# A planned attention-then-feed-forward kernel: two gate units in turns, one weights piece and the decays behind the second unit's rows, waiting engines, filler products and late fills

## The chip, the cores and the metric

The kernel runs on one core of a Trainium2 chip. The metric is the device time of one execution in microseconds. The kernel before took 734.04 us (median of 3 runs, 733.62 to 735.03).

## The reference

Two blocks follow each other. The first is a gated linear recurrence for 4 batches, 8 heads, 768 steps and head size 48; the second is a SwiGLU feed-forward on 3072 tokens of 384 features with a hidden width of 1536.

```python
mag = np.sqrt(a_re * a_re + a_im * a_im)
scale = np.minimum(mag, 0.999) / (mag + 1e-06)
a_re_n, a_im_n = (a_re * scale, a_im * scale)
for t in range(S):
    ar, ai = (a_re_n[:, :, t, :, None], a_im_n[:, :, t, :, None])
    new_re = ar * S_re - ai * S_im
    new_im = ar * S_im + ai * S_re
    kv = np.einsum('bhd,bhe->bhde', k[:, :, t], v[:, :, t])
    S_re, S_im = (new_re + kv, new_im)
    y[:, :, t] = np.einsum('bhd,bhde->bhe', q[:, :, t], S_re)
...
xn = x / np.sqrt(np.mean(x * x, axis=-1, keepdims=True) + 1e-06) * rms_g
g = xn @ w_gate
silu = g * (1.0 / (1.0 + np.exp(-g)))
return (silu * (xn @ w_val)) @ w_out
```

## The kernel before

The sequence is cut into 24 chunks of 128 steps (`N = 24`, n = 0 to 23). Chunks are grouped twice: into gate units (`UNITS`: chunk 0, chunk 1, then pairs) and into feed-forward groups of two chunks (`GROUPS`).

For a unit, `gates(u)` loads a_re and a_im (`load_gates`, tiles `in`) and q and k (`load_kq`, tile `kin`), works out in three stages ("size", "root", "turn") the running magnitude and angle of the decay (ScalarE table functions and VectorE scans over tiles `t`, `in`, `turns`), turns q and k by them into `rot`, and moves the rows of `rot` by six DMAs of 128 KB into a head-by-head layout, `kq`. Six small DMAs more move the chunk's end magnitudes, `ends`, into `decay`. `moved[n]` is the list of the row DMAs of chunk n.

For a chunk, `attend(n)` forms scores from `kq` on TensorE in small 32-column products (banks 4 and 5), masks them into `am` (`copy_predicated`), multiplies by v (`ve`) and by the carried state, and updates `state` with the chunk's decay. The stage "norm" squares the result (`sq`), sums it by a product with `ones`, takes the power -0.5 on GpSimd (`rs`), spreads it by another product, and writes `xT`, the normalised input of the feed-forward.

For a group, `feed(g, xT)` multiplies by w_gate (`wg`) and w_val (`wv`) in six blocks of 4 x 6 products, applies Silu on ScalarE (`sg`), multiplies on VectorE (`hT`), and multiplies by w_out (`wo`). From group 2 on the last product uses seven half-size products instead of eight (`weight_sums`).

The weights come in 64-bit words, as 12 pieces: 0 to 5 are w_gate and w_val in turns (1536 KB each), 6 to 11 are w_out (768 KB each). `fetch` loads a raw piece from GpSimd's DMA queue into free room in `wo` or `hT`; `narrow(i)` makes fp32 of it with one ScalarE instruction and three VectorE instructions. At most two pieces are in flight (`AHEAD`), the first waits until the gate inputs of unit 0 have landed (a one-element GpSimd copy, `junk`), and by `CLEAR = {3: 0}` piece 3 also waits until the rows of chunk 0 have landed (the copy `seen<-kq`).

Nothing of this is issued in program order. Each helper (`tt`, `act`, `dma`, `mms` and so on) only records an operation in `Flow`, with a planned duration and with what it reads and writes. `Flow.dates` works a due time backwards from the feed-forward products (`clock`), and `Flow.schedule` runs through time and gives every free engine, among the operations whose inputs are ready, the one due earliest. `behind` keeps a DMA's issue after that of others. The result is a fixed order for each engine, which `issue` writes out; all instructions therefore have line 648 in the profile, and they are told apart by their tiles. On the chip each engine takes its own list strictly in order, with the waits that reads and writes ask for. In the order that is written out, each DMA of the SP queue also waits until the one eight before it on the hardware queues has landed.

```python
key = o["due"]
if o["table"] and table not in self.TABLES[o["table"]]:
    key += self.switch
if pick is None or key < pick[0]:
    pick = (key, o)
```

The steps that the texts below speak of are found at `narrow` and `fetch` (pieces), `load_gates` and `load_kq` (inputs of a unit), `gates` with its last loop (the decays), `attend` with its "norm" stage, and the block of `fill` calls near the top of `fast` (constants and zeros, mostly on GpSimd). The names `kq`, `decay`, `am`, `state` in the profile leave out the buffer number: even chunks use the first buffer, odd chunks the second.

Of the kernel before, what the change touches and what calls it, by code (L numbers as in the profile page):

```python
# [19 lines left out]
C = 128  # L20
# [441 lines left out]
class Flow:  # L462
# [7 lines left out]
    LAND = 2.0  # L470
    LANES = 8
    BEGIN = {"SP": 0.8, "ACT": 0.8, "POOL": 0.8}
    TABLES = {"silu": ("S",), "sin": ("S", "T"), "arctan": ("T",), "rsqrt": ("A",)}

    def __init__(self, nc, rooms):
        self.nc = nc
        self.rooms = rooms
        self.ops = []
        self.seen = {}
        self.stage = None  # L480
        self.shift = {}

    def box(self, ap):
# [17 lines left out]
    def note(self, op, ap, write):  # L501
        b = self.box(ap)
        if b is None:
            return
        name, p0, p1, lo, hi = b
        if name.startswith("bank"):
            p0, p1, lo, hi = 0, P, 0, 2048
        kept = []
        for x in self.seen.get(name, ()):
            o, w, q0, q1, l, h = x  # L510
            over = q0 < p1 and p0 < q1 and l < hi and lo < h
            if over and (write or w) and o != op["i"]:
                op["deps"].add(o)
            if not (write and p0 <= q0 and q1 <= p1 and lo <= l and h <= hi):
                kept.append(x)
        kept.append((op["i"], write, p0, p1, lo, hi))
        self.seen[name] = kept

    def add(self, eng, calls, dur, reads=(), writes=(), table=None, land=None, due=None, after=(), behind=()):
        op = dict(i=len(self.ops), eng=eng, calls=calls, dur=dur, deps=set(), table=table, land=land,  # L520
                  base=due, stage=self.stage, behind={o["i"] for o in behind})
        self.ops.append(op)
        op["deps"].update(o["i"] for o in after)
        for ap in reads:
            self.note(op, ap, False)
        for ap in writes:
            self.note(op, ap, True)
        return op

    def dates(self):  # L530
# [15 lines left out]
        for op in self.ops:  # L546
            op["due"] += self.shift.get(op["stage"], 0.0)
        return users

    def schedule(self):  # L550
# [4 lines left out]
        waiting = {}  # L555
        table = None
        for op in self.ops:
            free.setdefault(op["eng"], self.BEGIN.get(op["eng"], 0.0))
            waiting.setdefault(op["eng"], [])
            if not left[op["i"]]:  # L560
                waiting[op["eng"]].append(op)
# [21 lines left out]
        while True:  # L583
# [26 lines left out]
            for o in waiting[eng]:  # L610
                if ready[o["i"]] > t + 1e-9:
                    continue
                key = o["due"]
                if o["table"] and table not in self.TABLES[o["table"]]:
                    key += self.switch
                if pick is None or key < pick[0]:
                    pick = (key, o)
            o = pick[1]
            waiting[eng].remove(o)
            dur = o["dur"]  # L620
            if o["table"] and table not in self.TABLES[o["table"]]:
                table = self.TABLES[o["table"]][-1]
                dur += 1.3
                self.loads = getattr(self, "loads", 0) + 1
            if eng == "PE":
                busy = sum(min(e, t) - max(b, t - 4.0) for b, e in recent if e > t - 4.0)
# [18 lines left out]
    def issue(self):  # L645
        for op in sorted(self.ops, key=lambda o: o["order"]):
            for fn, args, kw in op["calls"]:
                fn(*args, **kw)  # L648


def fast(tc, ctx, qT, kT, v, a_re, a_im, w_gate, w_val, w_out, rms_g, out, H, bad):
# [192 lines left out]
    for t, x in ((ones, 1.0), (halfpi, PI / 2), (mid, -(RE_MAX + RE_MIN) / 2),  # L844
                 (width, -(RE_MAX - RE_MIN) / 2), (mhalf, -0.5), (zeros, 0.0)):
        fill(t, x)
    for t in ves + states:
        fill(t[:, :, :, D:], 0.0)
    add("POOL", [(make_identity, (nc, ident), {})], 0.6, [], [ident])
    fill(causal, 1.0)  # L850
    for e in range(2):
        for b in range(4):
# [3 lines left out]
                                                            base=-BLK * (3 - b if e else b),  # L856
                                                            channel_multiplier=-1))], 0.3, [x], [x])
    for t in ams:
        fill(t, 0.0)
    for t in banks[4:6]:  # L860
# [21 lines left out]

    CLEAR = {3: 0}

# [61 lines left out]
    HOLD = 1  # L946
    begun = []
    cleared = {}
    loaded = {}
# [31 lines left out]
    def load_kq(u, t):  # L981
        flow.stage = "kq", u
        for name, ap in (("q", qT), ("k", kT)):
            for i, n in enumerate(UNITS[u]):
                dma(t[name][:, :, i * C:(i + 1) * C],
                    ap[n].rearrange("d (h t) -> (d h) t", t=C).rearrange("(j p) t -> p j t", p=P),
                    behind=moved[HOLD] if u > 1 else rows_)
        return t

    def gates(u):  # L990
# [45 lines left out]
        tt(q, q, t4)  # L1036

        flow.stage = "turn", u
        act(im, im, AF.Arctan, after=[root])
        last = turn.get(u - 1) if ns[0] % NCH else None  # L1040
# [16 lines left out]
        for i, n_ in enumerate(ns):  # L1057
            cs = slice(i * C, (i + 1) * C)
            for a, f in enumerate((t5, t3)):
                tt(rots[n_ % 2][:, a * ND:(a + 1) * ND].rearrange("p j (o t) -> p j o t", t=C), t["kq"][:, :, :, cs],  # L1060
                   f[:, :, cs].unsqueeze(2).to_broadcast([P, ND, 2, C]))
        for n_ in ns:
            moved[n_] = [dma(kqs[n_ % 2][r:D2:2 * ND], rots[n_ % 2][:, r], "SP") for r in range(2 * ND)]
            if n_ < 2:
                cleared[n_] = copy(seen, kqs[n_ % 2][:, 0, 0:1], eng="POOL")
        for r in range(2 * ND):
            dma(decays[way_of(u)][r:D2:2 * ND], ends[:, r % ND, ns[0]:ns[0] + nt], behind=moved[ns[0]])

# [9 lines left out]
    def attend(n):  # L1078
# [3 lines left out]
        vv = vns[0]  # L1082
        later = dict(behind=moved[min(n - 1, HOLD)] if n else ())
        rows = v[n * C:(n + 1) * C, :].rearrange("t (m e d) -> t m e d", e=2, d=D)
# [6 lines left out]
        for a in range(2):  # L1091
# [3 lines left out]
            for h in range(HH):  # L1095
                for b in range(4):
                    c = 3 - b if h % 2 else b
                    list_.append((s[c * BLK:(c + 1) * BLK, h, b * BLK:], k[:, a * HH + h, b * BLK:(b + 1) * BLK],
                                  q[:, a * HH + h, b * BLK:], True, True))
            mms(list_, HH // 2 * 0.29, due=EARLY.get(n))  # L1100
            pairs = lambda t: t.rearrange("s (m e) t -> s m e t", e=2)
# [21 lines left out]
        order = [lines[c][i] for i in range(len(lines[0])) for c in range(4)]  # L1123
        mms(order, len(order) * mm_time(C) / 4 * 1.1 + 0.15)
        if not last:
            kt = kts[0]
            for a in range(2):
# [8 lines left out]
            mms([(st[c * BLK:(c + 1) * BLK, h], kt[:, h, c * BLK:(c + 1) * BLK], vv[:, h], True, True)  # L1136
                 for h in range(H) for c in range(3)], H * 0.1)
            st4 = ps.rearrange("p (m e d) -> p m e d", m=NP, e=2)
# [44 lines left out]

    FIRST = 2
    B = {(k, j): wo[:, k * HD:(k + 1) * HD, j * DH:(j + 1) * DH] for k in range(2) for j in range(2)}
    blocks = lambda t: t.rearrange("p (f c) -> p f c", f=HD)
# [85 lines left out]
    for u in range(2):  # L1272
        load_kq(u, loaded[u])
    gates(0)
    gates(1)
    for i in range(len(pieces)):
        narrow(i)
    gated = 2
    for n in range(N):
        while gated < NU and UNITS[gated][0] <= n:  # L1280
            gates(gated)
            gated += 1
# [15 lines left out]
    for in_, limit, op in ((ef, P_MIN, ALU.is_ge), (ef, 1.0, ALU.is_le), (range_, 0.0, ALU.is_le),  # L1298
# [12 lines left out]
        0.2, [ps[0:1, 0:1]], [], due=clock[0] - 15.0)  # L1311

    flow.schedule()
    with tc.manual_schedule():
# [51 lines left out]
```

## Time and profile before

| what | value |
|---|---|
| median of 3 runs | 734.04 us |
| profiled execution, its own time | 735.44 us |
| its span from first to last instruction | 733.7 us |
| TensorE busy | 679.7 us (93%) |
| VectorE busy | 473.2 us (64%) |
| ScalarE busy, of it 68 table loads | 331.3 us, 87.2 us |
| GpSimd busy | 42.0 us |
| moved by DMA | 80.64 MB |

A row of the profile gives engine, operation, output tile and input tiles, and shape; times are from the start of the span. "SPq" and "POOLq" are the DMA-issuing instructions of the queues. In the timeline the number in front is the start, the next one the length, and a bracket tells how long the engine had been idle before and what released it. In a window row each engine has its busy microseconds and, in brackets, its instructions; PEclk is TensorE's granted clock, the last two columns are the share in use of the 16 DMA engines and GB/s. A TensorE product of fp32 is two records in the profile.

### The profile page before, as it was taken

What the parts mean: (1) busy time and instruction counts of PE and PEld (TensorE: products, weight loads), DVE (VectorE), ACT (ScalarE), POOL (GpSimd) and SP (SyncE); (2) the same over time, 40 slices, a digit from 0 to 9 for tenths busy, and PEclk for the clock granted to TensorE, in tenths of its full rate; (3) what the DMA queues carried; (4) which work ended last, traced back from release to release, by engine and by line L of the source; (5) the groups of instructions that cost most, each with busy time, mean ns of one, the idle gap of its engine ahead of it and who ended that gap; (6) DMA issues with size and microseconds to landing.
All of it is one profiled execution on the core that took longest, in us unless ns stands there. A gap on an engine that the chain in (4) does not pass through costs nothing.

```text
span 733.7 us, 16076 instructions
## 1 busy us (share of the span) xinstructions
PE 679.7 (93%) x6842; PEld 598.6 (82%) x6842; DVE 473.2 (64%) x740; ACT 331.3 (45%) x451; POOL 42.0 (6%) x80
## 2 busy tenths in 40 slices
PE   0269989999999999999999999999999999999996
PEld 0257866877888889889889889889889889889885
DVE  6979897789798887886856745765845233234121
ACT  7646856867384742841832732731830110111010
POOL 5122200000000000000000001000000000000000
PEclk9978999999999999999999999999999999999999
DMA  8597675544756625643523303313303202200000
GB/s 296 186 318 211 163 178 160 140 128 110 195 129 152 177 84 139 215 145 78 151 66 77 119 22 73 113 34 79 106 1 77 66 13 67 65 12 3 22 0 27
DMA packets 104575, 80.64 MB, mean 110 GB/s; under 512 B 42800, under 2 KB 95280, under 8 KB 104496
## 3 DMA queue, kind: packets, MB, share of 16 engines
q1 hardware_dynamic: 100432, 64.99, 33.2%
q0 software_dynamic: 3264, 14.16, 5.6%
q8 instruction: 56, 0.92, 0.5%
q10 hardware_dynamic: 800, 0.39, 0.2%
q14 instruction: 23, 0.19, 0.1%
HBM read 55.84 MB, written 4.72 MB: 83 GB/s over the span
## 4 chain that ended last, share of the span: by engine, by line
PE 64%; DVE 2%; DMA 2%; SPq 2%; ACT 1%; issue 0%; DVEq 0%; ACTq 0%
PE bank L648 64%; SPq L648 2%; DMA kq<-rot 1%; DMA in<-in_a_im_dram 1%; DVE turns L648 0%; DVE t L648 0%; ACT turns L648 0%; DVE hT L648 0%; DVE large L648 0%; DVE xT L648 0%; DVE in L648 0%; ACT L648 0%; DVE small L648 0%; DVE ot L648 0%; DVE rot L648 0%
## 5 line engine op out<-in xcount | busy, mean ns | idle before, releaser
L648 PE MATMUL bank<-xT,wg 128*128 128x256 f32 x864 | 200.8, 382 | 2.8 <-DVE xT L648 2.8
L648 PE MATMUL bank<-xT,wv 128*128 128x256 f32 x864 | 199.0, 380 | 0.0
L648 PEld LDWEIGHTS bank<-xT,wg 128*128 128x128 f32 x864 | 164.4, 191 | 25.9 <-DVE xT L648 3.5
L648 PEld LDWEIGHTS bank<-xT,wv 128*128 128x128 f32 x864 | 163.6, 190 | 22.5
L648 PE MATMUL bank<-wo,hT 128*128 128x192 f32 (+1 forms) x576 | 124.8, 360 | 0.5 <-DVE hT L648 0.4
L648 DVE TENSOR_TENSOR hT<-bank,sg 128x512 f32<-128x512 f32 x72 | 49.4, 687 | 108.6 <-PE bank L648 104.9
L648 PEld LDWEIGHTS bank<-wo,hT 128*128 128x128 f32 x576 | 94.6, 190 | 14.2 <-issue 1.4
L648 ACT ACTIVATE sg<-bank 128x512 f32<-128x512 f32 x72 | 42.8, 595 | 133.3 <-PE bank L648 132.9
L648 ACT ACT_TABLE_LOAD x68 | 87.2, 1283 | 16.3 <-DVE rot L648 8.6
L648 PE MATMUL bank<-kq 96*32 96x96 f32 (+3 forms) x1536 | 35.5, 243 | 33.8 <-DVE wg L648 28.2
L648 PEld LDWEIGHTS bank<-kq 96*32 96x32 f32 x1536 | 31.7, 114 | 39.7 <-DVE wg L648 28.2
L648 DVE TENSOR_TENSOR rot<-kin,turns 128x768 f32<-128x768 f32 x48 | 44.9, 953 | 18.4 <-DMA kq<-rot 17.5
L648 ACT ACTIVATE sq<-bank 128x384 f32<-128x384 f32 x24 | 11.7, 487 | 96.5 <-PE bank L648 95.8
L648 POOL TENSOR_TENSOR rs<-ssv,mhalf 128x1 f32<-128x1 f32 x24 | 18.4, 766 | 573.1 <-DVE ssv L648 573.1
L648 ACT ACTIVATE kt<-bank 128x384 f32<-128x384 f32 x40 | 18.4, 486 | 64.4 <-PE bank L648 63.6
L648 PE MATMUL bank<-sums,hT 128*128 128x192 f32 x240 | 45.2, 330 | 0.0
L648 PE MATMUL bank<-am,ve 128*32 128x128 f32 x768 | 41.4, 290 | 0.4 <-DMA ve<-in_v_dram 0.4
L648 PEld LDWEIGHTS bank<-sums,hT 128*128 128x128 f32 x240 | 39.4, 190 | 0.4 <-DVE mid L648 0.3
L648 DVE TENSOR_TENSOR hT<-hT 128x768 f32<-128x768 f32 x40 | 38.2, 954 | 0.9
L648 DVE COPY_PREDICATED am<-causal,bank 128x512 f32<-128x512 int32 x48 | 32.9, 720 | 8.1 <-PE bank L648 8.1
L648 ACT ACTIVATE turns<-in 128x768 f32<-128x768 f32 (+1 forms) x39 | 29.9, 789 | 14.8 <-DVE in L648 11.0
L648 PE MATMUL bank<-kq,state 96*32 96x128 f32 x640 | 35.6, 285 | 0.0
(110 smaller groups left out, 715.6 us busy)
## 6 DMA issues: line engine op xcount, KB each, us to landing
kq<-rot SPq DMA_DIRECT2D x144, 128.0 KB, 2.4
kin<-in_q_dram SPq DMA_DIRECT2D x24, 192.0 KB, 3.1
kin<-in_k_dram SPq DMA_DIRECT2D x24, 192.0 KB, 4.4
wo<-in_w_gate_dram SPq DMA_DIRECT2D x6, 768.0 KB, 4.4
out_dram<-ot SPq DMA_DIRECT2D x24, 192.0 KB, 2.2
wo<-in_w_val_dram SPq DMA_DIRECT2D x6, 768.0 KB, 5.0
wo<-in_w_out_dram SPq DMA_DIRECT2D x6, 768.0 KB, 4.7
in<-in_a_re_dram SPq DMA_DIRECT2D x11, 384.0 KB, 4.5
```

What stands on the lines that cost most here:

```text
L648: fn(*args, **kw)
```

## The change

- **Gates in turns.** `gates` becomes a generator that stops once, after the root stage. For units 0 and 1 the first part of both is recorded, then the second part of both; the angle function (`Arctan`, another table) of each waits for the roots of both.
- **Piece 3 behind the second rows.** `CLEAR` is `{3: 1}`: the fourth weights piece waits for the rows of chunk 1 instead of chunk 0.
- **Decays behind the second rows.** The decay DMAs of units 0 and 1 are recorded after unit 1's rows and placed behind them in the SP queue; those of later units follow their own unit's second rows (`send_decays`).
- **Waiting engines.** When the planner has picked an operation for ScalarE or VectorE, and one due over 50 us earlier becomes ready within 1.5 us, while the picked one would still run, the engine idles until then.
- **Fillers.** Up to 62 us of planned time, gaps of TensorE are filled with products of 128 x 128 by 128 from the first `rot` into bank 3, after the first `rot` instruction. 38 of them are issued: 16 ahead of the scores of chunk 0, 7 and 8 around the second half of the scores of chunk 1, and 2, 4 and 1 in the norm stage of chunk 1.
- **Late fills.** Fills of `ve`, `state`, `am`, the mask and the identity are due no earlier than 12 us.
- **Planner details.** Loads of q, k and v of one unit or chunk do not count as dependent on each other (`group`); a change between product shapes costs 0.06 us of planned time (the rate for ordering by it, `turn`, stays 0); two planned durations of products are changed.

The program contains the same operations otherwise, in a new order on every engine. On VectorE the two units' first parts now stand ahead of the first `rot`, and between the masks of chunk 0 and those of chunk 1 the order is: piece 1, one of the three instructions of piece 2, `state<-bank,decay`, the other two of piece 2. On ScalarE the list before the squares of chunk 1 holds the first instruction of unit 2 (`t<-in`) and the conversion of piece 3, in that order. The program has as many table loads as before.

```diff
+            if eng in self.patient:
+                for x in waiting[eng]:
+                    if t < ready[x["i"]] < t + o["dur"] - 0.2 and x["due"] < o["due"] - 50.0 and ready[x["i"]] < t + 1.5:
+                        pick = None
+                        free[eng] = max(free[eng], min(ready[y["i"]] for y in waiting[eng] if t < ready[y["i"]]))
+                        break
+                if pick is None:
+                    continue
...
+            if eng == "PE" and o["mode"] != mode:
+                mode = o["mode"]
+                dur += 0.06
+            if eng == "PE" and self.warm and t < self.warm["until"]:
+                since = max([free["PE"]] + [x["end"] + self.SYNC for x in self.warm["after"] if not recent])
+                n = int((t - since - 0.3) / 0.43)
+                if n > 0:
+                    self.fillers.append((order - 0.5, n))
+                    recent.append((since, since + 0.43 * n))
...
+    LATE = 12.0
     for t in ves + states:
-        fill(t[:, :, :, D:], 0.0)
+        fill(t[:, :, :, D:], 0.0, late=LATE)
...
-    CLEAR = {3: 0}
+    CLEAR = {3: 1}
...
+    def send_decays(u):
+        ns = UNITS[u]
+        for r in range(2 * ND):
+            dma(decays[way_of(u)][r:D2:2 * ND], ends[:, r % ND, ns[0]:ns[0] + len(ns)], behind=moved[max(ns[0], 1)])
...
+        roots.append(root)
+        yield
         flow.stage = "turn", u
-        act(im, im, AF.Arctan, after=[root])
+        act(im, im, AF.Arctan, after=roots[-2:])
...
-        for r in range(2 * ND):
-            dma(decays[way_of(u)][r:D2:2 * ND], ends[:, r % ND, ns[0]:ns[0] + nt], behind=moved[ns[0]])
+        if u:
+            for x in (u - 1, u) if u == 1 else (u,):
+                send_decays(x)
...
-            mms(list_, HH // 2 * 0.29, due=EARLY.get(n))
+            mms(list_, HH // 2 * 0.285, due=EARLY.get(n), mode=BLK)
...
-        mms(order, len(order) * mm_time(C) / 4 * 1.1 + 0.15)
+        mms(order, len(order) * mm_time(C) / 4 * 1.06, mode=BLK)
...
-    gates(0)
-    gates(1)
+    firsts = [gates(0), gates(1)]
+    for x in firsts * 2:
+        next(x, None)
...
+    filler = rots[0][:, 0]
+    flow.warm = dict(after=started, until=WARM, call=[
+        (nc.tensor.matmul, (banks[3][:, 0:C],), dict(lhsT=filler[:, 0:C], rhs=filler[:, C:2 * C], start=True, stop=True))])
```

## The prediction

> **What bounds the kernel now.** First the page's busy shares by slice and what TensorE waited for:
>
> ```profile
> PE   0269989999999999999999999999999999999996
> ```
>
> ```profile
> PE bank L648 <- DVE wg L648: 28.2, 1, 28.2
> PE bank L648 <- DMA kq<-rot: 5.6, 2, 4.8
> PE bank L648 <- DVE am L648: 5.2, 2, 3.2
> ```
>
> From the fourth slice on TensorE is full; all its long waits are before. So whatever brings the start of the full stretch forward moves the end with it, as long as nothing behind goes empty. (The wait of 28.2 us is put down to `wg`, but the copy `seen<-kq` begins at 28.20: the rows of chunk 0 ended it.) Then the windows, with busy time of PE, PEld, DVE, ACT, POOL, PEclk, DMA share, GB/s:
>
> ```profile
> 25.00:30.00 5.00, 1.78 (x56) 1.81 (x60) 4.96 (x6) 2.88 (x8) 0.44 (x1) 1.00 0.37 89
> 40.00:45.00 5.00, 1.04 (x32) 1.07 (x36) 3.52 (x3) 1.63 (x1) 2.23 (x4) 0.65 0.96 299
> 45.00:50.00 5.00, 4.56 (x86) 3.79 (x81) 4.18 (x6) 0.49 (x1) 1.65 (x3) 0.50 1.11 293
> 55.00:60.00 5.00, 3.51 (x53) 2.99 (x54) 4.96 (x6) 4.79 (x8) 1.83 (x2) 0.52 0.55 112
> 80.00:85.00 5.00, 5.00 (x25) 4.38 (x25) 4.98 (x7) 4.96 (x8) 1.68 (x3) 1.00 0.37 91
> 95.00:100.00 5.00, 3.87 (x74) 2.25 (x72) 5.00 (x8) 3.26 (x4) 0.00 (x0) 1.00 0.82 220
> ```
>
> DMA is idle around 25 to 30 and full from 40 to 50; TensorE's clock is half there; VectorE is full from 55 to 100, while TensorE runs feed 0. Then single steps, in the timelines:
>
> ```profile
> 33.03 4.18 SPq L648 DMA_DIRECT2D kq<-rot  x6
> 43.96 2.36 PE L648 MATMUL bank<-kq 96*32 96x128 f32 x64 [4.78 <-DMA kq<-rot]
> 50.27 0.84 ACT L648 ACTIVATE t<-in 128x768 f32<-128x768 f32 x1 [2.58 <-DMA in<-in_a_re_dram]
> 58.65 3.62 PE L648 MATMUL bank<-xT,wg 128*128 128x256 f32 x8
> 90.95 1.82 DVE L648 TENSOR_TENSOR rot<-kin,turns 128x768 f32<-128x768 f32 x2
> 98.01 1.33 PE L648 MATMUL bank<-kq 96*32 96x128 f32 x64 [0.82 <-DMA kq<-rot]
> 101.83 0.55 PE L648 MATMUL bank<-ident,kq 96*128 96x96 f32 x4 [2.01 <-DVE am L648]
> ```
>
> Chunk 1's rows, issued up to 37.2, land at 43.9, while piece 3 (POOLq from 30.83) flows. Feed 0 starts at 58.65. At 98.0 TensorE waits for unit 2's rows, which VectorE finished in `rot` at 92.77: **from 58 to 98 VectorE, not TensorE, sets the pace**, and a feed 0 that starts earlier pays only as far as `rot` of unit 2 comes earlier.
>
> **What the skill says.** (1) "TensorE: Matmul & The Clock Gate", What's actually happening: after some 3.4 us of idleness the clock halves, and as long a busy time restores it. The trace agrees: the 64 score products took 2.36 us at 43.96 and 1.33 us at 98.01. (2) "DMA: Bandwidth & Descriptors", Issuing engines are not separate DMA queues: all queues share the 16 engines and interleave. It agrees: the 12 row DMAs of 20 to 50 us took 2.2 to 7.6 us to land, the slow ones beside a piece. (3) "SBUF — State Buffer", Who interferes with whom: a two-port VectorE operation and GpSimd block each other. It agrees: two 384-element TENSOR_SCALARs took 1.46 us at 8.54, one took 0.33 at 11.08; GpSimd was filling until 10.04.
>
> **The change, part by part**, on the execution with a span of 733.7 us.
>
> *Gates in turns, to the rows of chunk 0.* ScalarE starts at 4.72 as before, but the square of unit 0's a_im is now behind five instructions instead of two: three more at some 0.42 us each, and one dependent gap. On VectorE 0.96 + 0.56 + 0.51 of unit 1 stand before unit 0's scans, so these end at about 12.1 (before 11.16). Roots and square: 12.2 to 13.7, one table load to 15.0 (before two, 12.30 and 14.13), angle of unit 0 at 15.0 (13.59). Then VectorE: two corrections, two `kin`, scan, two corrections of unit 1, one step to 18.3, with the conversion of piece 0 (1.6) on ScalarE until 18.8; magnitude 0.5, load 1.28, sine and cosine 1.0: 21.6 (20.03). First `rot` 22.6 to 23.5 (22.02 before), second to 24.4 (24.34, since no unit 1 step lies between). Six row DMAs at 0.68 each from 23.6: the last is issued at 27.0 (25.6), rows land at **29.6 (28.2): a loss of 1.4**. The late fills cost nothing: GpSimd ends its fills near 10.1 as before, and VectorE's TENSOR_SCALAR now comes after that, which saves the 0.8 us lost at 8.54; that is in the dates above. The first wait for ACT's inputs moves by 0.2 (the table load now precedes the DMAs), hidden behind a_re, which ScalarE waits for until 4.72.
>
> *Rows of chunk 1.* VectorE's `rot` of unit 1 ends at 30.2 (before 33.9). SP has `kq` 0 until 27.6, four `ve` until 30.2, then six rows until 34.3 (before 37.2). Nothing of 1.5 MB flows beside them, so 2.5 us after the last issue, as with chunk 0: **36.5 against 43.9, a gain of 7.4**.
>
> *Decays.* Queued behind the rows: six from 34.9 to 38.8, landing after 1.8 to 5.9 us (the spread of the 12 of before): 41 is taken, 44 the upper end. `state<-bank,decay` waits for them on VectorE, free at 38.4; behind it are queued 1.76 + 1.76 of piece 2 and the masks of chunk 1: these end at 46.4 (before 47.1). So 6 of the 7.4 are lost again here.
>
> *Piece 3.* It waits on GpSimd's queue, where piece 4 (at 38.3, before 39.11) and the powers (from 45) stand behind it and lose nothing. Issued at 36.9 (30.83), landed by a rate as before (9.5 us): 46, at most 49. Unit 2's a_re is issued at 38.9 (41.14) and takes 9.1 us as before: 48. ScalarE stands at its first instruction for this, 0.84, then the conversion of piece 3, 1.6: the square of chunk 1 can start at 50.4 (53.16). Its result y, masks at 46.4, power product and 2 us at a warm clock (114.47 to 116.4; cold it took 4.8), is ready at 48.9, so the input sets the date. From the square 0.5, sum 0.7, `ssv` 0.2, power 0.7 to 1.2, product 0.5, `xT` 0.55 and handovers: **feed 0 starts at 54.2 (58.65): 4.4 earlier**; 52.3 if a_re lands at 46, 56 if at 50.
>
> *Fillers.* A record of 128x256 takes 2.75/12, less its tail, 0.216 warm, 0.43 cold; a filler is two records half as wide, 0.22 warm, 0.43 cold. The first 16 end between 27.1 and 30.5, 29.0 taken, ahead of the rows (29.6): at worst 0.9 on a path that has slack at `decay`. Those between scores fill waits. What they gain is in y above (2.8 of 4.8); feed 0 also lost 1.7 by the clock (91.46 - 58.65 less 72 x 0.432), but that is before VectorE's date and counts nothing.
>
> *VectorE from `xT` to `rot` of unit 2.* In before 57.74 to 92.77: 35.0. The list after is the same less one `hT` product (0.6), plus the first two instructions of piece 4 (0.95 + 1.76), which were done earlier: 33 us of lengths if nothing is waited for, 34.8 with a wait for a_im of unit 2 until 55. So `rot` 102 ends at 87.3 to 88.9, mean 88.3 against 92.77; rows land 5.2 later, at 93.5 (98.0). TensorE gets there at 92.1: block and w_out products are reordered so that the first `hT` of 74 holds nothing up. From there `am` follows 8.4 after `rot` (8.3 before), so the gap of 2 us stays.
>
> *The rest.* The place of the scores of later chunks among the feed products is the same or up to 28 us of products later, for every chunk; TensorE's gaps after 130 sum to some 4 us and I take them as unchanged, +-1.5. Waiting engines and planner details act only through these orders: zero taken, -1.5 to +1.5. The group of loads: zero, inputs of unit 2 are in the dates above.
>
> Sum: loss 1.4 + gain 7.4 - lost behind the decays and a_re = 4.4 at feed 0; 4.4 kept at 88.3; less 0.4 for waits on w_out pieces, which are issued as late as before (the seventh at 61.3 against 60.88) and meet an earlier VectorE: **4.0 us**. Span 729.7, execution 731.4 (1.7 around the span); the profiled execution was 1.4 above the median, so the median goes from 734.04 to **730.0**.
>
> **Rivals.**
> *Transfers come earlier than I put them* (0.12): a_re at 46 and decays at 40, feed 0 at 52 and no wait of VectorE: `rot` near 85.5, gain 7: 727. For it: DMA moved 375 GB/s at 50 to 55; against: 293 at 45 to 50.
> *VectorE was the bound throughout* (0.23): work before 98 is the same, holes only move, gain 0 to 2.4: 733. For it: 4.96 of 5 in most windows. Against: it idles 1.5 at 40 to 45 and 2.8 at 50 to 55, waiting for chunk 1.
> *Slower* (0.15): piece 3 moves 1.5 MB out of the idle DMA stretch into the full one; at 299 GB/s that is 5.1 us for everything behind it: a_im of unit 2, pieces 4 and 5, then w_out. VectorE meets them in order; once its waits from 54 to 88 sum to over 4.4 + 1.5, `rot` is later than before. If each of piece 5 and three w_out pieces costs 2 us, 8: 737. Against: piece 5 needs to be there at 64, expected at 58.
> That the change does nothing is excluded only for the rows' date; the fillers may fail to lift the clock: 2.8 at y, of which 1.3 shows, inside the range.
>
> **Numbers.** As worked, 728 to 731.5: 0.50; better 0.12; little or nothing 0.23 (0.10 of it faster by over 0.2%, 1.5 us, about what a measurement tells from no change); slower 0.15. Faster 0.72, same 0.13, slower 0.15. Range 726 to 735.
>
> **What would show it.** Rows of chunk 1 landed at 36 to 38; VectorE idle before `state<-bank,decay`; ScalarE idle before `t<-in` until 48; feed 0 at 52 to 56; `rot` of unit 2 at 87 to 90; scores of chunk 2 near 93.5; TensorE gaps after 130 as before. It is wrong if waits for `wo`, `hT` or `in` on VectorE between 54 and 88 sum to over 4 us, or a new gap of TensorE opens after 100.

## The result and the profile after

The changed kernel takes 736.06 us (median of 10 runs, 734.83 to 737.85) against 734.26 us before (10 runs): this by before is 1.0025, 95% interval 1.0011 to 1.0039. It is slower by 0.25%. The prediction was 730.0, a gain of 4.

The profiled execution of the changed kernel took 735.34 us with a span of 733.6; that of the kernel before took 735.44 with 733.7. So the profiled pair is level where the medians are 1.8 apart: the profile of before happens to be 1.2 above its median, that of after 0.7 below. What follows compares stretches inside the spans; it can show why the gain of 4 didn't come, but not where the 1.8 between the medians lie.

First the page of the kernel after: TensorE's busy tenths in 40 slices.

```profile
PE   0568979999999999999999999999999999999996
```

And what its matrix products waited for (total us, times, longest us):

```profile
PE bank L676 <- DVE rot L676: 23.2, 1, 23.2
PE bank L676 <- DVE state L676: 6.5, 1, 6.5
PE bank L676 <- DMA kq<-rot: 3.2, 3, 1.6
```

The second slice went from 2 to 5 and the wait of 28.2 us ends at 23.2: that is the fillers, which do no work for the output. A new wait of 6.5 us, for `state`, lies in the third slice; the fourth and the sixth are a tenth lower than before. The full stretch starts no earlier.

The windows of the kernel after, columns as before (PE, PEld, DVE, ACT, POOL, clock, DMA share, GB/s):

```profile
35.00:40.00 5.00, 3.63 (x46) 3.40 (x46) 3.09 (x3) 0.16 (x1) 2.49 (x3) 0.71 0.42 81
40.00:45.00 5.00, 0.76 (x5) 0.57 (x3) 0.00 (x0) 0.00 (x0) 0.00 (x0) 0.84 1.00 389
45.00:50.00 5.00, 2.78 (x39) 2.69 (x40) 2.81 (x3) 0.00 (x0) 0.00 (x0) 0.50 1.06 348
60.00:65.00 5.00, 4.51 (x14) 3.56 (x14) 4.83 (x5) 3.99 (x4) 0.00 (x0) 0.66 0.26 44
95.00:100.00 5.00, 4.93 (x19) 3.04 (x17) 4.96 (x8) 0.94 (x1) 1.36 (x2) 1.00 1.03 345
```

From 40 to 45 no engine but TensorE does anything, and the DMA engines are full (share 1.00, 389 GB/s): everybody waits for a transfer. At 60 to 65, in the first products of feed 0, the clock is 0.66 in spite of the fillers. From 95 to 100 the DMA share is 1.03, where it was 0.82.

The timelines of the kernel after (start, length, engine, and in brackets the idle time ahead and its releaser):

```profile
36.64 0.98 PE L676 MATMUL bank<-kq 96*32 96x128 f32 x32 [1.37 <-DMA kq<-rot]
35.44 4.77 SPq L676 DMA_DIRECT2D decay<-ends  x6
37.24 1.13 POOL L676 DMA_DIRECT2D wo<-in_w_val_dram  x1
38.37 0.77 POOL L676 DMA_DIRECT2D wo<-in_w_gate_dram  x1
46.62 0.55 DVE L676 TENSOR_TENSOR state<-bank,decay 96x384 f32<-96x384 f32 x1 [8.49 <-DMA decay<-ends]
55.21 0.50 ACT L676 ACTIVATE sq<-bank 128x384 f32<-128x384 f32 x1
57.33 2.00 POOL L676 TENSOR_TENSOR rs<-ssv,mhalf 128x1 f32<-128x1 f32 x1 [4.55 <-DVE ssv L676]
60.59 1.75 PE L676 MATMUL bank<-xT,wg 128*128 128x256 f32 x4 [0.49 <-DVE xT L676]
93.90 1.83 DVE L676 TENSOR_TENSOR rot<-kin,turns 128x768 f32<-128x768 f32 x2
101.70 1.33 PE L676 MATMUL bank<-kq 96*32 96x128 f32 x64 [1.56 <-DMA kq<-rot]
```

The rows of chunk 1 land at 36.6 (before 43.9). The six decay DMAs are issued behind them, from 35.44 to 40.2, and pieces 3 and 4, 3 MB together, are issued at 37.24 and 38.37 into the same stretch. VectorE stands for 8.49 us at `state`, until 46.62. Behind it the masks and the norm of chunk 1 are late, feed 0 starts at 60.59 (58.65), `rot` of unit 2 ends at 95.73 (92.77), the scores of chunk 2 start at 101.7 (98.0).

VectorE takes its list in order, so the end of `rot` of unit 2 is a plain sum: the start of the count, plus its busy time, plus its idle time. From 12 us to that end, the kernel before:

```profile
12.00:92.77 80.77, 53.28 (x501) 45.79 (x502) 69.92 (x89) 54.92 (x75) 16.10 (x25) 0.89 0.77 230
```

and the kernel after:

```profile
12.00:95.73 83.73, 60.15 (x574) 52.46 (x575) 67.55 (x87) 50.24 (x71) 16.39 (x24) 0.92 0.68 215
```

VectorE's busy time (third engine column) fell from 69.92 to 67.55, by 2.37, and its idle time rose from 80.77 - 69.92 = 10.85 to 83.73 - 67.55 = 16.18, by 5.33. The difference is the 2.96 us by which `rot` is later. One wait makes up 8.5 of the 16.2.

Behind 130 us something is won. Windows of before:

```profile
130.00:400.00 270.00, 267.04 (x2714) 234.59 (x2714) 213.29 (x331) 152.59 (x195) 7.35 (x9) 1.00 0.49 133
```

and of after:

```profile
130.00:400.00 270.00, 269.95 (x2730) 237.32 (x2729) 212.49 (x327) 154.88 (x198) 8.71 (x10) 1.00 0.47 133
```

TensorE's idle time there falls from 2.96 to 0.05. With 3.0 lost before and 2.9 won behind, the two spans are level.

### The profile page after: what moved, and what is told of

It is laid out like the page before. It is cut to its first block, busy times and chain, and to the rows that moved or that the text cites. A ratio compares the mean times of both kernels' runs of the same rounds, so it can differ in the third digit from the quotient of the medians.

```text
span 733.6 us, 16218 instructions
## 1 busy us (share of the span) xinstructions
PE 685.9 (93%) x6918; PEld 604.2 (82%) x6918; DVE 472.1 (64%) x740; ACT 333.1 (45%) x451; POOL 47.4 (6%) x80
## 4 chain that ended last, share of the span: by engine, by line
PE 84%; DVE 5%; ACT 2%; issue 2%; DMA 2%; SPq 1%; POOL 1%; DVEq 0%; POOLq 0%; ACTq 0%
PE bank L676 84%; SPq L676 1%; DMA decay<-ends 1%; DMA hT<-in_w_out_dram 1%; DVE turns L676 1%; DVE t L676 1%; DVE wo L676 1%; ACT t L676 1%; POOL junk L676 1%; ACT turns L676 1%; ACT L676 1%; DVE rot L676 0%; DMA in<-in_a_re_dram 0%; DVE hT L676 0%; DVE wg L676 0%
## 5 line engine op out<-in xcount | busy, mean ns | idle before, releaser
L676 PEld LDWEIGHTS bank<-xT,wg 128*128 128x128 f32 x864 | 164.3, 191 | 24.4 <-DVE xT L676 1.9
L676 POOL TENSOR_TENSOR rs<-ssv,mhalf 128x1 f32<-128x1 f32 x24 | 20.1, 839 | 574.4 <-DVE ssv L676 574.4
L676 ACT ACTIVATE kt<-bank 128x384 f32<-128x384 f32 x40 | 18.4, 489 | 73.5 <-PE bank L676 54.5
L676 PEld LDWEIGHTS bank<-kq 96*32 96x32 f32 x1536 | 30.2, 111 | 16.4 <-issue 8.5
L676 PE MATMUL bank<-kq 96*32 96x128 f32 (+3 forms) x1536 | 34.6, 238 | 9.7 <-DVE state L676 6.5
L676 ACT ACTIVATE turns<-in 128x768 f32<-128x768 f32 (+1 forms) x39 | 30.1, 789 | 16.2 <-DVE in L676 13.8
L676 PE MATMUL bank<-am,ve 128*32 128x128 f32 x768 | 37.1, 275 | 0.0
L676 PE MATMUL bank<-rot 128*128 128x128 f32 x76 | 14.0, 356 | 23.2 <-DVE rot L676 23.2
```

## The experiments

The theory after the result: the decays are the step that failed. Queued behind the second rows they land behind the start of pieces 3 and 4, and `state`, which stands in VectorE's list ahead of everything chunk 1 needs, waits for them. The rivals: the piece behind the second rows; a second wait that stands right behind the first (piece 3's conversion on ScalarE, ahead of the squares of chunk 1); the fillers; the waiting engines; the turns.

Two kinds of kernels were run. In the first (names with e and f) the planned order of the changed kernel is kept on every engine, and only the steps named are put elsewhere by setting their `order` after `flow.schedule()`. For an added line of code the profile's line is 677 instead of 676. In the second kind (p and q) the source is changed and the planner runs again, so that the order of many steps changes. None leaves out a part of the computation. The ratio is to the kernel before on the same chip in the same job; the changed kernel was timed in a job of its own, so that it is compared with the others through these ratios. The dates of each kernel are those of one profiled execution, which need not be a middle one: that of `e4_piece_first` took 3.1 us more than the kernel's median, that of `q1_before_clear1` 3.5 us less, the others at most 1.7 off.

| kernel | feed 0 starts | `rot` of unit 2 ends | VectorE busy, idle since 12 | of it at `state` | time, this / before | ratio, 95% |
|---|---|---|---|---|---|---|
| before | 58.65 | 92.77 | 69.92, 10.85 | 0 | | |
| after | 60.59 | 95.73 | 67.55, 16.18 | 8.5 | 736.06 / 734.26 | 1.0025, 1.0011 to 1.0039 |
| e1_decays_sp | 59.10 | 94.67 | 67.97, 14.70 | 0 | 734.16 / 734.97 | 0.9997, 0.9985 to 1.0010 |
| e2_decays_act | 59.94 | 95.16 | 67.93, 15.23 | 0 | 734.63 / 734.97 | 0.9991, 0.9970 to 1.0011 |
| e3_piece_last | 61.04 | 96.83 | 67.75, 17.08 | 3.3 | 735.91 / 734.97 | 1.0020, 1.0007 to 1.0034 |
| e4_piece_first | 57.28 | 93.25 | 67.74, 13.51 | 4.7 | 734.47 / 734.97 | 0.9996, 0.9978 to 1.0014 |
| f1_both_waits | 53.61 | 91.34 | 67.93, 11.41 | 0 | 731.99 / 734.59 | 0.9978, 0.9964 to 0.9991 |
| f2_piece3_late | 59.44 | 97.17 | 67.67, 17.50 | 9.0 | 737.78 / 733.91 | 1.0048, 1.0028 to 1.0068 |
| e5_no_fillers | 60.97 | 96.68 | 67.49, 17.19 | 6.7 | 737.99 / 734.59 | 1.0054, 1.0031 to 1.0078 |
| p1_clear0 | 61.30 | 93.80 | 68.13, 13.67 | 8.5 | 735.71 / 734.59 | 1.0010, 0.9994 to 1.0026 |
| p2_decays_before | 51.90 | 92.49 | 67.90, 12.59 | 0 | 730.55 / 734.59 | 0.9950, 0.9932 to 0.9967 |
| p3_impatient | 62.13 | 104.8 | 68.4, 24.4 | 10.1 | 749.18 / 733.91 | 1.0204, 1.0179 to 1.0229 |
| p4_no_turns | 59.12 | 97.30 | 69.20, 16.10 | 5.6 | 739.14 / 733.91 | 1.0058, 1.0032 to 1.0083 |
| q1_before_clear1 | 57.24 | 92.67 | 69.42, 11.25 | 0 | 734.29 / 733.91 | 1.0004, 0.9979 to 1.0028 |

**The decays ahead again, on the SP queue and on ScalarE's queue.**

```diff
+    for i, x in enumerate(sent_[0]):
+        x["order"] = moved[0][-1]["order"] + 0.01 * (i + 1)
```

> The kernel after, with the six decay DMAs of chunk 0 moved in the SP queue from behind the rows of chunk 1 to right behind the rows of chunk 0; every other list keeps its order. Theory A (the decays land late because they flow beside pieces 3 and 4, and VectorE stands at state for 8.5 us): the wait at state goes, the rows of chunk 1 land some 4 us later (near 40.5), feed 0 starts near 57 instead of 60.6, and the time falls by 2 to 4 us. Theory B (pieces and VectorE's work set the pace, the wait at state only fills a hole that would be there anyway): within 1 us of the kernel after. Theory C (holding piece 3 back is the loss): no gain, or a loss, since the rows that piece 3 waits for come later still.

For ScalarE's queue the same DMAs are issued by ScalarE behind its conversion of piece 2, which takes them out of the SP queue:

```diff
+    for i, x in enumerate(sent_[0]):
+        x["order"] = lows[2]["order"] + 0.01 * (i + 1)
+        x["calls"] = [(nc.scalar.dma_start, a, k) for _, a, k in x["calls"]]
```

> The kernel after, with the six decay DMAs of chunk 0 issued from ScalarE's queue, behind the conversion of piece 2, where ScalarE idles for 3.4 us; the SP queue loses them and nothing else moves. Theory A: decays land by 34, rows of chunk 1 at 36.6 as after, state at 38, feed 0 near 54, and the time falls by 4 to 5 us, to 731 to 732, below the kernel before. Theory B: feed 0 moves by less than 2 us, since ScalarE then waits for a_re of unit 2 or piece 3, and the time stays within 1 us. Theory C: no gain.

In both the wait at `state` is gone (it runs at 38.3 without idle time, 8.3 us earlier). The time falls from 0.25% above before to no difference that can be told. The 8 us are hardly passed on: feed 0 starts 1.5 us (`e1_decays_sp`) and 0.7 us (`e2_decays_act`) earlier than after, where theory A had 3.6 and 6.6. For `e2_decays_act` theory B had this date right (under 2 us). The timelines of `e2_decays_act` show who is late next:

```profile
38.26 0.55 DVE L677 TENSOR_TENSOR state<-bank,decay 96x384 f32<-96x384 f32 x1
38.91 0.77 PE L677 MATMUL bank<-kq 96*32 96x128 f32 x32 [3.43 <-DMA kq<-rot]
40.46 0.78 POOL L677 DMA_DIRECT2D wo<-in_w_val_dram  x1
50.95 0.96 DVE L677 TENSOR_SCALAR wv<-wo 128x1536 int32<-128x1536 int32 x1 [4.03 <-DMA wo<-in_w_val_dram]
51.98 1.77 ACT L677 ACTIVATE wo<-wo 128x1536 int32<-128x1536 uint32 x1 [4.71 <-POOL junk L677]
53.63 0.51 ACT L677 ACTIVATE sq<-bank 128x384 f32<-128x384 f32 x1
```

TensorE has the products that the squares of chunk 1 take as their input done by 48.2 here, and ScalarE is free from 47.3. But piece 3's conversion stands ahead of the squares in its list and waits 4.71 us for the piece (VectorE waits 4.03 for it). The squares start at 53.63 (55.21 after). A second wait takes the place of the first. In part the edit makes it: with the decays ahead, the second rows are later (their scores start at 38.91 here and at 40.62 in `e1_decays_sp`, 36.64 in after), and piece 3, which waits for these rows, is issued at 40.46 and 41.14 instead of 37.24.

**Both waits off, and the second alone.** Piece 3's conversion and its three VectorE instructions go behind `xT` of chunk 1, once with the decays on ScalarE's queue and once with the decays as in the changed kernel.

```diff
+    at = xts[1]["order"]
+    lows[3]["order"] = at + 0.1
+    for i in range(3):
+        flow.ops[nar[3][0] + i]["order"] = at + 0.2 + 0.1 * i
```

> The kernel after with both waits ahead of feed 0 taken off its path: the decays of chunk 0 go out on ScalarE's queue as in e2, and the conversion of piece 3 (one ScalarE and three VectorE instructions) is moved behind the norm stage of chunk 1, so that neither ScalarE nor VectorE stands for piece 3 before xT. Theory A2 (two waits lay side by side, and taking one away only showed the other; the start of the full stretch still sets the end): feed 0 near 52 to 53 (after 60.6), the second power no longer lengthened to 2 us by the piece, rot of unit 2 4 us earlier or more, time near 731. Theory B (from 58 to 98 pieces and VectorE's work set the pace): feed 0 near 52 too, but rot of unit 2 not before 92, and the time within 1.5 us of the kernel before.

> The changed kernel's order with one hand-made move: the ScalarE conversion of piece 3 and its three VectorE instructions stand behind xT of chunk 1, while the decays stay behind the second rows. Two waits in a row (decays, then piece 3): the decays still hold state on VectorE until about 46.6, masks end near 52, so the squares of chunk 1 start at 53.6 instead of 55.2 (the conversion of 1.6 is gone from ahead of them) and feed 0 at about 58.5 instead of 60.6; time 735 to 736, within 0.2% of before. Rival (the piece's conversion ahead of the squares is the whole loss): feed 0 at 54 and time about 732.

With both off, the timelines of `f1_both_waits`:

```profile
48.19 0.49 ACT L677 ACTIVATE sq<-bank 128x384 f32<-128x384 f32 x1 [1.01 <-PE bank L677]
51.78 0.57 POOL L677 TENSOR_TENSOR rs<-ssv,mhalf 128x1 f32<-128x1 f32 x1
53.61 4.53 PE L677 MATMUL bank<-xT,wg 128*128 128x256 f32 x12 [0.49 <-DVE xT L677]
```

and its window to the end of `rot` of unit 2:

```profile
12.00:91.34 79.34, 61.75 (x583) 53.63 (x584) 67.93 (x88) 50.61 (x71) 18.49 (x24) 0.96 0.73 233
```

Feed 0 starts at 53.61 (52 to 53 expected), 7 us earlier than after; VectorE's idle time is 11.41, 4.8 less than after; `rot` ends at 91.34, 4.4 earlier; the time is 0.22% below before. That is the size that the prediction had for the whole change at this place: feed 0 at 54.2. Theory B, with `rot` not before 92, falls.

With the second wait alone off (`f2_piece3_late`) nothing is gained. What its VectorE waited for in the same stretch:

```profile
DVE state L677 <- DMA decay<-ends: 9.0, 1, 9.0
DVE ssv L677 <- PE bank L677: 3.2, 1, 3.2
```

The wait for the decays stays, and the 4.5 us of piece 3 on VectorE (0.96 + 1.76 + 1.75), which had lain ahead of `xT`, now lie behind it: `rot` ends at 97.17, later than after. Feed 0 was expected at 58.5 and came at 59.44; the time was expected at 735 to 736 and is 737.78, a miss to the slow side. The rival that had the whole loss in that conversion (732) falls. So the two waits are in series, and each edit alone gives little: 1.0025 with neither removed, 0.9991 with the decays' alone, 1.0048 with the conversion's alone, 0.9978 with both. (The intervals of 0.9991 and 0.9978 overlap; it is the profiles that tell those two apart, with feed 0 at 59.94 and 53.61.)

**Where piece 3 stands.** Pieces 3 and 4 held until the decays have landed too, by a copy of one element that waits for them; then piece 3 ahead of the wait for the second rows.

```diff
+    at = max(cleared[1]["order"], sent_[0][-1]["order"])
+    raws[3]["order"], raws[4]["order"] = at + 0.2, max(raws[4]["order"], at + 0.3)
+    flow.extra.append((at + 0.1,
+                       [(nc.gpsimd.tensor_copy, (), dict(out=seen, in_=decays[0][:, 0, 0:1]))]))
```

> The kernel after, with pieces 3 and 4 held until the decays of chunk 0 have landed too (one more one-column GpSimd copy that waits for them). Theory A: without pieces beside them the decays land near 42 instead of 46.6, but the pieces start near 42 instead of 37.2 and are 4 us later: feed 0 about as after or up to 2 us earlier, time from -2 to +1. Theory B and C (pieces set the pace): slower by 2 to 4 us.

The timelines of `e3_piece_last`:

```profile
41.57 0.55 DVE L677 TENSOR_TENSOR state<-bank,decay 96x384 f32<-96x384 f32 x1 [3.32 <-DMA decay<-ends]
42.12 0.78 POOL L677 DMA_DIRECT2D wo<-in_w_val_dram  x1 [0.35 <-DVE state L677]
52.08 0.96 DVE L677 TENSOR_SCALAR wv<-wo 128x1536 int32<-128x1536 int32 x1 [3.11 <-DMA wo<-in_w_val_dram]
```

This measures the disputed cost: with no piece beside them, the same six decays at the same place in the queue are ready at 41.57, where the prediction had them at 41. Beside the two pieces they are ready at 46.62. The two pieces cost them 5.1 us. The time is no better, 1.0020, which is within what theory A had: the piece that is now later, from 42.12, ends the next wait. A loss of 2 to 4 us against after (theories B and C) isn't there.

```diff
+    cleared[1]["order"] = raws[3]["order"] + 0.1
```

> The kernel after, with piece 3 again ahead of the wait for the rows of chunk 1 on GpSimd's queue, as before; piece 4 still behind it. Theory A: rows of chunk 1 land near 43 and the decays behind them near 46 as well, so the wait at state stays or grows; within 1.5 us of the kernel after. Theory C (holding piece 3 back is the loss): faster by about 2 us, back to the kernel before.

Theory A had the wait at `state` stay or grow, and that was a miss: it falls to 4.7 us. Feed 0 comes at 57.28, 3.3 earlier than after, and the time, 0.9996, can't be told from before, which is the number of theory C. So moving the piece ahead gives back as much as moving the decays ahead (0.9997), and these two runs alone don't tell which of them stood in the wrong place; `p2_decays_before`, below, does. In the profiled execution TensorE then waits 5.5 us for the rows of unit 2, beside two w_out pieces (both issued from 88.8), and the scores of chunk 2 start at 103.2, later than after. Whether that wait is there in the usual execution isn't shown, since this one is 3.1 us above the median.

**Parts of the change undone.** All are planned anew except the fillers, which are left out of the planned order.

```diff
-    CLEAR = {3: 1}
+    CLEAR = {3: 0}
```

> The kernel after planned anew with piece 3 behind the rows of chunk 0 as before (CLEAR = {3: 0}); all other parts of the change stay. If the wait of piece 3 is what loses (theory C): back at the kernel before or faster, by 1 to 3 us against after; feed 0 near 56. If the decays' place is (theory A): still about as after, with the decays landed near 43.

The decays are waited for as long (8.5 us, `state` at 48.58, where 43 was expected for them), since here too they have a piece beside them (piece 4, issued at 37.96), and feed 0 is no earlier (61.30). The time, 1.0010 (0.9994 to 1.0026), can't be told from before or from after. So piece 3 ahead of the second rows doesn't by itself bring the front back. The other way round, that edit alone in the kernel before:

```diff
-    CLEAR = {3: 0}
+    CLEAR = {3: 1}
```

> The kernel before, planned again with piece 3 behind the rows of chunk 1 and nothing else of the change. Piece behind the rows is a gain by itself: rows of chunk 1 land near 39.7 instead of 43.9 (last issue 37.2 plus 2.5), piece 3 near 48.5, feed 0 at 55 to 57, time 731 to 733. Rival (the piece only moves its 1.5 MB into the full stretch and is met there by VectorE): rows land early but rot of unit 2 ends as before at 92 to 93, time 734 to 736. The order of chunk 1's norm relative to unit 2's first steps is planned anew, which can hide either by 1 to 2 us.

Gain or loss can't be told: 734.29 against 733.91, with single runs from 729.8 to 740.0. Feed 0 comes 1.4 earlier, at 57.24, and `rot` of unit 2 ends at 92.67, as in before: this is what the rival had.

```diff
-            dma(decays[way_of(u)][r:D2:2 * ND], ends[:, r % ND, ns[0]:ns[0] + len(ns)], behind=moved[max(ns[0], 1)])
+            dma(decays[way_of(u)][r:D2:2 * ND], ends[:, r % ND, ns[0]:ns[0] + len(ns)], behind=moved[ns[0]])
...
-        if u:
-            for x in (u - 1, u) if u == 1 else (u,):
-                send_decays(x)
+        send_decays(u)
```

> The kernel after planned anew with the decays of each unit behind the unit's own first rows as before; all other parts of the change stay, piece 3 behind the second rows among them. Theory A2: the wait at state goes, the wait for piece 3 stays, so feed 0 at 58 to 60 and the time from -2 to 0 against after. Theory A as first stated: feed 0 near 55 and -4.

This is the version that beats both kernels: 730.55 us, 0.9950 of before (0.9932 to 0.9967), with every part of the change except the decays. It is faster than either theory expected, with feed 0 at 51.90 instead of 55 or 58 to 60. `p1_clear0` made the opposite choice, the piece early and the decays late, and its interval lies wholly above this one. So neither piece 3 behind the second rows nor the late fills and the planner details, which were not undone one by one, keep the rest from gaining. Its timelines:

```profile
27.32 3.81 SPq L676 DMA_DIRECT2D decay<-ends  x6
34.77 0.55 DVE L676 TENSOR_TENSOR state<-bank,decay 96x384 f32<-96x384 f32 x1
37.45 1.43 PE L676 MATMUL bank<-kq 96*32 96x128 f32 x64 [2.24 <-DMA kq<-rot]
47.25 0.49 ACT L676 ACTIVATE sq<-bank 128x384 f32<-128x384 f32 x1 [3.36 <-PE bank L676]
48.80 1.65 ACT L676 ACTIVATE wo<-wo 128x1536 int32<-128x1536 uint32 x1
51.90 2.86 PE L676 MATMUL bank<-xT,wg 128*128 128x256 f32 x12 [0.27 <-DVE xT L676]
```

The decays are never waited for, and the second rows are only 0.8 us later than after (scores at 37.45 instead of 36.64). That is not the whole price of the decays' place: in `e1_decays_sp`, with every other list unchanged, it was 4.0 us (40.62). Here the new plan also issues the loads of `ve` behind the second rows (from 35.66) instead of ahead of them (27.05 in after). The planner, with the decays out of the way, also puts piece 3's conversion (48.80) behind the squares (47.25) by itself. Feed 0 starts at 51.90 and warm: 2.86 us for its first 12 records, against 4.5 in before, after and `f1_both_waits`. (The warm start alone is no gain: `f2_piece3_late` has it too, 2.86.) Of its 8.7 us against after, `rot` of unit 2 passes on 3.2; in between TensorE stands empty for `hT` (1.83 and 1.58 us) and for VectorE's conversion of a w_out piece (2.02). VectorE sets the pace there, as the prediction said.

```diff
+    flow.fillers = []
```

> The kernel after without its 38 filler products; the order of everything else is kept. If the fillers help: y of chunk 1 takes 4 us instead of 2, feed 0 starts 1 to 3 us later and its first products are as cold as after (12 records in 4.5 us), time +0.5 to +2. If they don't help, because the waits (decays, piece 3) cover TensorE's slower steps: within 0.7 us. If they hurt (they are in front of urgent products): up to 1 us faster.

Without fillers 1.0054 against 1.0025 with them; the intervals overlap by a little, so that some 2 us for them is likely and not certain. The products that make y of chunk 1, its result ahead of the norm, took 3.65 us (1.96 with fillers), close to the 4 expected, but feed 0 came only 0.4 later, not 1 to 3. Two lines of the timeline show the slow products of chunk 1 (eight records in 0.66 us, in 0.40 with fillers) and the cold start of feed 0 (5.10, where 4.5 was expected):

```profile
51.33 0.66 PE L677 MATMUL bank<-am,ve 128*32 128x128 f32 x8
60.97 5.10 PE L677 MATMUL bank<-xT,wg 128*128 128x256 f32 x12 [0.72 <-DVE xT L677]
```

```diff
-    patient = ("ACT", "DVE")
+    patient = ()
```

> The changed kernel planned anew without the rule that lets ScalarE and VectorE idle for an urgent operation; decays still behind the second rows. Theory (decays behind the second rows set the date of chunk 1): VectorE still waits for them until 45 to 47, feed 0 at 58 to 62, time 735 to 737. Rival (the idle engines are the loss): feed 0 by 56, time about 732.

The decays are waited for 10.1 us, as expected, but the time, 749.18, is far above the 735 to 737 expected. VectorE's list to `rot` of unit 2 is about as long (68.4), but it idles for 24.4 us: up to 60 us 18.4 (13.8 after), at `state`, at `ssv` (5.9) and elsewhere, and 6.0 behind (2.4 after), with `rot` of unit 2 at 104.8. Neither theory had that. It says that the waiting engines are no loss in this plan; it doesn't say what they are worth in another.

```diff
-    for x in firsts * 2:
-        next(x, None)
+    for x in firsts:
+        list(x)
...
-        act(im, im, AF.Arctan, after=roots[-2:])
+        act(im, im, AF.Arctan, after=[root])
```

> The changed kernel planned anew with the gates of unit 0 and unit 1 one after the other; decays still behind the second rows, one table load more. Theory: rows of chunk 0 land near 28.2 again and those of chunk 1 near 40, three to four later than with turns; decays behind them land later too, near 48 to 50; feed 0 at 61 to 63, time 736 to 738, above the changed kernel. Rival (turns cost more than they bring, since the rows of chunk 0 are later by 0.9): time below the changed kernel, 734.

1.0058, above the changed kernel's 1.0025, though the intervals overlap by a little. The dates in between were missed: the rows of chunk 0 land at 29.1 and those of chunk 1 at 37.2, not 28.2 and 40, and feed 0 came at 59.1 instead of 61 to 63. VectorE's list to `rot` of unit 2 is 1.65 us longer than with turns (69.20 against 67.55), with the same idle time. That the turns lose, the rival, is not borne out.

## Why the prediction was wrong

By its own steps:

- *Rows of chunk 0*, 29.6: measured 29.1. *Rows of chunk 1*, 36.5: measured 36.6. *Fillers* ended at 29.0: 28.8. These steps held.
- *Decays*, "landing after 1.8 to 5.9 us (the spread of the 12 of before): 41 is taken, 44 the upper end": measured 46.6. **This is the step that failed.** The landing times were taken from a stretch in which the decays had one piece beside them or none. The prediction itself moved piece 3 to 36.9 and left piece 4 at 38.3, exactly into these transfers, and wrote 46 for the landing of the piece, but did not give the decays the same traffic. `e3_piece_last` gives 41.57 without the pieces, so the rest, 5.1 us, comes from their company. The landing times in the profile of after are 1.8 to 7.8 us, median 4.7.
- *Piece 3 loses nothing for what stands behind it.* Right as put, but its conversion stands ahead of the squares of chunk 1 and waits for it as soon as the decays don't (`e2_decays_act`, 4.71 us, with the piece itself 3.2 us later than in after). The prediction had the conversion in its sum with its length only, because its late input was `in`. In the changed kernel itself it cost little, since the decays were later.
- *Square to feed 0*: predicted 50.4 to 54.2, 3.8; measured 55.21 to 60.59, 5.4. The power on GpSimd was taken at 0.7 to 1.2 and took 2.00, since a VectorE conversion of piece 3 (57.15, 1.75 us, two inputs) runs beside it and the power ends 0.4 behind it. The Trainium skill, "SBUF — State Buffer", Who interferes with whom, says that the one that comes second is blocked for the whole of the other's instruction; the prediction cited that section and did not apply it here.
- *VectorE from feed 0 to `rot` of unit 2*: predicted 54.2 to 88.3, 34.1; measured 60.59 to 95.73, 35.1. That **VectorE sets the pace between 58 and 98** held: in all the kernels with hand-moved steps its list is 67.5 to 68.0 us, so that almost only its idle time dates `rot`.
- The sum at `rot`: 95.73 - 88.3 = 7.4 too early, of it 4.8 at the square of chunk 1 (50.4 against 55.21: the decays' 5.6 less the 1.5 that y was to lie idle for a_re, and 0.7 of small terms), 1.6 from there to feed 0, 1.0 behind it.
- *Gaps after 130 unchanged, +-1.5*: in the profiled pair TensorE's idle time from 130 to 400 falls by 2.9, nearly twice the bound. This was luck: it made up for the 3.0 lost ahead of it, and without it the span, forecast at 729.7 and measured at 733.6, would have been near 736.5. A new plan alone can do it: `q1_before_clear1`, which changes one number in the kernel before, has 0.65 us of idle time there.
- *a_re at 48 as the next date behind the rows*: not visible, since ScalarE stood until 52.5 for the masks of chunk 1, which the decays held up.
- *Two slips in the working*, without weight for the result: in the third point of "What the skill says" the 1.46 us at 8.54 are one TENSOR_SCALAR, not two, so that the effect is larger than stated; and with y ready at 48.9, feed 0 could not be earlier than 52.7, where 52.3 is given for an a_re at 46.

The rivals: *slower* had the sign and not the mechanism. It put the waits between 54 and 88, at piece 5 and the w_out pieces, and wanted over 5.9 us of them; VectorE waits there for `ssv`, `xT` and `hT` alone, 4.0 us, and from 60 on it idles 2.35 us in all, where it idled 2.70 in before. The loss lies ahead, at `state`. *VectorE bound throughout* had the gain lost because VectorE was never idle; in fact it was idle 5.3 us longer. What the change promised, 7 us at the second rows, arrived there, and was taken back one step later by transfers that it had itself put into each other's way.

## What to carry to other kernels

When transfers are moved, make a list of all that then flows at the same time, and give each of them the landing time of a stretch that is as full, not of the stretch it came from. A few small transfers that an in-order engine waits for go ahead of the large ones: here 3.8 us of queue ahead of the second rows took away a wait of 8.5. They are not free: the rows came 4.0 later where nothing else was moved, and 0.8 later where the plan was made anew around them. And where an edge is taken away, look in each engine's list for what stands between the wait and the urgent step: here two waits in series paid fully only when both were gone.

## What was not expected of the hardware

- The same six small DMAs, issued over 4.6 to 4.8 us, were ready 1.3 us after the last issue had ended with no piece beside them (`e3_piece_last`, 40.26 to 41.57) and 6.4 us after it beside two pieces of 1.5 MB from another queue (46.62 after 40.2). The Trainium skill, "DMA: Bandwidth & Descriptors", Issuing engines are not separate DMA queues, has the queues interleave on the same engines; that agrees, and this is its price here.
- GpSimd's power of 128 x 1 took 0.57 us in the changed kernel's first norm and 2.00 in the second, where it met a VectorE conversion; in `f1_both_waits`, with VectorE idle, 0.57. The same conversion, moved away, leaves the power at 0.56 in `f2_piece3_late`. A copy of one element took 4.64 us, over several VectorE instructions that followed each other without a gap, against 0.17 for others. The timeline of the kernel after:

```profile
51.33 0.57 POOL L676 TENSOR_TENSOR rs<-ssv,mhalf 128x1 f32<-128x1 f32 x1 [12.19 <-DVE ssv L676]
59.29 0.17 POOL L676 COPY junk<-wo 1x1 int32<-1x1 int32 x1
98.81 4.64 POOL L676 COPY junk<-hT 1x1 int32<-1x1 int32 x1 [2.45 <-DMA hT<-in_w_out_dram]
```

- The clock fell as feed 0 began, though TensorE had no long wait. In the kernel after, from 57.55 to 60.96, TensorE was busy for 1.50 of 3.41 us at a clock of 1.00, with no single wait over 1.42; from 62 to 64 the clock was 0.50. The prediction's "some 3.4 us of idleness" doesn't cover this. In `f2_piece3_late`, with the same fillers, TensorE was busy for 2.80 of the 3.40 us from 56.20 to 59.60, and from 60 on the clock stayed at 1.00.
